# The second transform stage as four 64x64 TensorE tiles, with both filter products summed in PSUM

## The chip, the cores and the metric

The kernel runs on one core of one Trainium2 chip. The metric is the device time of one execution in microseconds, as the median of several runs. The engines named here are TensorE (PE, with its weight loads as PEld), VectorE (DVE), ScalarE (ACT), GpSimd (Pool) and SyncE (SP).

## The reference

The input `x` has 8 sequences of 3008 positions and 256 channels. Each channel is filtered along the sequence in the frequency domain, and every filtered position then goes through a two-layer MLP.

```python
def _attn_ref(x, filt_r, filt_i):                 # x (8, 3008, 256), filters (1505, 256)
    X = np.fft.rfft(x, axis=1)
    F = (filt_r + 1j * filt_i)[None, :, :]
    return np.fft.irfft(X * F, n=x.shape[1], axis=1).astype(np.float32)

def _moe_ref(x, w_in, w_out):                     # x (24064, 256), d_ff 2048
    h = x @ w_in
    return (np.maximum(0.01 * h, h) @ w_out).astype(np.float32)
```

## The kernel before

**The transform.** 3008 = 94 x 32. The real transform of a sequence is done in two stages of matmuls. Stage one (`s1_group`) multiplies the 94 rows of each of 32 positions `n2` with a twiddled matrix. Its output has four groups of 32 partitions: the real and imaginary parts for two halves of the 48 first-stage frequencies, 24 used partitions of 32 in each. A transpose of 32x32 blocks on DVE (`t1_part`) turns the layout, so that the 32 positions lie on partitions and the 24 frequencies on the free axis. Stage two (`s2_group`) multiplies this with `fwd2`, a 128x128 matrix. Only entries that join real and imaginary parts of one half of the frequencies are nonzero in it: two interleaved 64x64 blocks.

The spectrum is multiplied with the filter straight out of PSUM. `p1` is the spectrum times the real filter `fa`. `p2` takes the other half of the partitions (real and imaginary parts exchanged) times the imaginary filter `fb`. Pool adds the two into `y1`. The inverse runs the same way back: `sa_group` multiplies with `inv2` (128x128), ACT casts the result into the next layout (`spread`, L181), `t2_part` transposes on DVE, and `sb_group` multiplies with the inverse matrix of stage one and copies to `yts`, which is already the transposed input of the MLP.

**The MLP.** 47 chunks of 512 tokens. `moe1_group` (L365) fills one two-bank PSUM tile `ph` with four matmuls of 512 columns, and ACT applies the leaky ReLU (L370). `moe2_slice` (L379) makes eight matmuls of 256 columns into `po_ps`; after every second slice ACT copies the output (L386) and SP stores it.

**PSUM.** Two tiles `ph` of two banks, three tiles `pf` of one bank, one bank `po_ps`: all eight. `bank("pf", ...)` hands out the three `pf` tiles in turn, to every transform stage.

**Order.** The schedule is written out by hand. A slot is one `moe1_group`, then the transform work that is listed for that slot, then one `moe2_slice` of the chunk before:

```python
for slot in range(SL * (NCHUNK + 1)):
    ci, g = divmod(slot, SL)
    if ci < NCHUNK:
        moe1_group(ci, g)
    for f in tasks.get(slot, ()):
        f()
    if ci > 0:
        moe2_slice(ci - 1, g)
```

`plan` spreads the transform of batch b+1 over the slots of batch b. Its last arguments for the second stage are the first slot `s2`, the pace `step` in quarters of a slot, and `lag`, the slots between a group's forward part and its inverse part. Batch 1 has step 4, the others step 5, all lag 3. Each engine runs its instructions in the order in which the code issues them.

**The first batch** has no MLP work to hide behind. Its transform is done in two halves of the channels (`hf`), with functions of its own (`first_s1`, `first_s2`, `first_sa`, `first_t2`, `first_sb`). There both products already go to the inverse separately: `first_sa` multiplies one with `inv2` and the other with `inv2x` into one accumulation. Part of the products is made on Pool from ACT's copies of the spectrum, the rest on DVE. `upper` (L308) copies the filter from the lower 64 partitions to the upper 64, for one half of the channels: `fa` on ACT, `fb` on DVE. `first_sb` (L301) works in tiles of 64 columns, in pairs. `keep_warm` (L313) issues matmuls whose result nobody reads. Once the first batch is through, Pool flips the sign of the upper half of `fb` (L347), as the later batches want it.

**DMAs.** Pool's queue carries `x`, the filters (`filt_load`, L140) and the weights, one after another; SP's carries the constants and the output.

Of the kernel before, what the change touches and what calls it, by code (L numbers as in the profile page):

```python
# [10 lines left out]
P = 128  # L11
FP16 = mybir.dt.float16
# [7 lines left out]
NC = 24  # L20
Q = 32
# [4 lines left out]
def _build_np_constants(N):  # L26
    n1, n2 = np.arange(N1), np.arange(N2)
    h = N2 // 2

    k2 = np.concatenate([np.arange(h), np.arange(N2 - 1, h - 1, -1)])  # L30

    sg = np.where(k2 < h, 1.0, -1.0)[None, :]
    th = 2 * np.pi * np.outer(n2, k2) / N2
    co, si = np.cos(th), np.sin(th)

    fwd1 = np.zeros((R1, N2, P))
    inv1 = np.zeros((P, N2, N1))
    fwd2, inv2 = np.zeros((P, P)), np.zeros((P, P))

    for s, (qr, qi) in enumerate(((0, 2), (1, 3))):  # L40
        k1 = NC * s + np.arange(NC)

        w = np.where((k1 == 0) | (k1 == N1 // 2), 1.0, 2.0)[:, None] / N1
        for j in n2:
            ang = 2 * np.pi * (np.outer(n1, k1) / N1 + j * k1[None, :] / N)
            fwd1[:N1, j, qr * Q : qr * Q + NC] = np.cos(ang)
            fwd1[:N1, j, qi * Q : qi * Q + NC] = -np.sin(ang)
            inv1[qr * Q : qr * Q + NC, j, :] = w * np.cos(ang).T
            inv1[qi * Q : qi * Q + NC, j, :] = -w * np.sin(ang).T

        cr, ci = (slice(64 * i + s, 64 * i + 64, 2) for i in range(2))
        r, i = (slice(Q * q, Q * q + Q) for q in (qr, qi))
        fwd2[r, cr], fwd2[i, cr] = co, si
        fwd2[r, ci], fwd2[i, ci] = -si * sg, co * sg
        inv2[cr, r], inv2[ci, r] = co.T, -(si * sg).T
        inv2[cr, i], inv2[ci, i] = si.T, (co * sg).T
    inv2 /= N2

    inv2x = np.concatenate([inv2[64:], -inv2[:64]], axis=0)
    small = np.stack([fwd2, inv2, inv2x], axis=1)  # L60
    fwd1 = fwd1.reshape(R1, FP, N2 // FP, P).transpose(1, 0, 2, 3)
    return (np.ascontiguousarray(fwd1).astype(np.float16), inv1.astype(np.float16), small.astype(np.float16))
# [3 lines left out]
def kernel(  # L66
# [16 lines left out]
    CH = 512  # L83
# [12 lines left out]
    small_sb = cpool.tile([P, 3, P], FP16, name="small_sb")  # L96
    fa_sb = cpool.tile([P, NC, D], FP16, name="fa_sb")
    fb_sb = cpool.tile([P, NC, D], FP16, name="fb_sb")
# [8 lines left out]
    ypp = ctx.enter_context(tc.tile_pool(name="ypp", bufs=4))  # L107
# [98 lines left out]
    def s2_group(b, g):  # L206
        def go():
            ps = bank("pf", 2, D)
            src = big[(4 * b + 1) % 3][:].rearrange("p (n d) -> p n d", n=Q)
            nc.tensor.matmul(ps, fwd2, src[:, ds(2 * g, 2), :], start=True, stop=True)  # L210
# [5 lines left out]
            nc.vector.tensor_tensor(p2[64:P], ps[0:64], fb[0:64], AL.mult)  # L216
            y1 = ypp.tile([P, 2, D], FP16, tag="y", name=f"y_b{b}_g{g}")
            nc.gpsimd.tensor_tensor(y1[:], p1[:], p2[:], AL.add)  # L218
            ys[(b, g)] = y1
        return go  # L220

    def sa_group(b, g):
        def go():
            ps = bank("pf", 2, D)
            nc.tensor.matmul(ps, inv2, ys.pop((b, g))[:], start=True, stop=True)  # L225
            spread(big[(4 * b + 2) % 3], 2 * g, ps, nc.scalar.copy)
        return go
# [28 lines left out]
    def first_s2(hf, c, n, on_pool):  # L256
        ps = bank("ph", n, DH)
        src = paired(big[1])
        for j in range(0, n, 4):
            nc.tensor.matmul(ps[:, ds(j, 4), :].rearrange("p n (e t) -> p n e t", t=2), fwd2,  # L260
                             src[:, ds(c + j, 4), ts(hf, DH // 2)], start=True, stop=True)
        fs = [f[:, ds(c, n), ts(hf, DH)] for f in (fa_sb, fb_sb)]
        if on_pool:
            y = [outp.tile([P, n, DH], FP16, tag="ost", name=f"fy{i}_h{hf}_c{c}") for i in range(2)]
            xs = [scrp.tile([P, 4, DH], FP32, tag=f"p{j // 4 + 1}", name=f"fx_h{hf}_c{c + j}")
                  for j in range(0, n, 4)]
            for j, xf in enumerate(xs):
                act(xf[:], ps[:, ts(j, 4), :])
            for i in range(2):
                for j, xf in enumerate(xs):  # L270
                    nc.gpsimd.tensor_tensor(y[i][:, ts(j, 4), :], xf[:], fs[i][:, ts(j, 4), :], AL.mult)
        else:
            y = [ypp.tile([P, n, DH], FP16, tag=f"yw{i}", bufs=2, name=f"fy{i}_h{hf}_c{c}")
                 for i in range(2)]
            for i in range(2):
                nc.vector.tensor_tensor(y[i][:], ps, fs[i], AL.mult)  # L276
        ys[(hf, c)] = y

    def first_sa(hf, c):
        y = ys.pop((hf, c))  # L280
        for j in range(0, y[0].shape[1], 4):
            ps = bank("pf", 4, DH)
            for i, m in enumerate((inv2, inv2x)):
                nc.tensor.matmul(ps, m, y[i][:, ds(j, 4), :], start=(i == 0), stop=(i == 1))  # L284
            act(paired(big[2])[:, ds(c + j, 4), ts(hf, DH // 2)],
                ps.rearrange("p n (t e) -> p n e t", t=2))
# [18 lines left out]

    def upper(hf):
        for t, cp in ((fa_sb, act), (fb_sb, dve)):
            cp(t[64:P, :, ts(hf, DH)], t[0:64, :, ts(hf, DH)])  # L308


    def keep_warm(n):
        for _ in range(n):
            nc.tensor.matmul(po_ps.rearrange("p a d -> p (a d)"), small_sb[:, 0, :],  # L313
                             i1_sb[:].rearrange("p a d -> p (a d)")[:, 0:512],
# [31 lines left out]

    nc.gpsimd.tensor_scalar(fb_sb[64:P], fb_sb[64:P], -1.0, None, AL.mult)  # L347
# [51 lines left out]
    def plan(b, s1, per, t1, s2, step, lag, t2, sb):  # L399
# [57 lines left out]
```

## Time and profile before

| what | before |
|---|---|
| median of three runs | 785.82 us (785.38 to 785.87) |
| the profiled execution, own time | 787.67 us |
| its span | 785.9 us |
| mean granted TensorE clock | 0.997 |
| TensorE busy | 763.0 us, 97% |
| ACT busy | 557.0 us, 71% |
| DVE busy | 365.1 us, 46% |
| Pool busy | 150.7 us, 19% |
| first MLP matmul (L365) | 45.56 us after the start |

The profile is of one execution, in microseconds from the start of its span. Busy time is the sum over an engine's instructions. A line such as "L210 PE MATMUL ... x84 | 31.8, 379 | 0.0" is a group: source line, engine, operation, written and read tiles, count, then busy time in us, mean ns of one, and the idle time of the engine just before them. A matmul's duration is its whole flight through the array; the next one starts before it ends. In the timeline a row is the start, the duration, the engine, the line and the operation; neighbours of one kind are merged, and a bracket tells the idle time before and what ended it.

### The profile page before, as it was taken

Reading aid. Unit: us, or ns where it says so; the run is one execution under the profiler, and the core shown is the slowest. Engines: PE = TensorE matmul, PEld = TensorE weight load, DVE = VectorE, ACT = ScalarE, POOL = GpSimd, SP = SyncE. Lnnn points to the kernel's source line nnn. Section 1 sums busy time; section 2 is a strip of 40 time slices with the busy share of each in tenths; the row PEclk is TensorE's granted clock in tenths of the full one; section 3 lists DMA queues with packets and bytes.
Section 4 is the critical chain, followed back from the end, with each engine's and each line's share of the span. In section 5 each row is a group of like instructions: output and inputs, shape, how many; then the busy total and the mean of one; then the engine's idle time right before and its main releaser. Section 6 shows DMA issues by size and latency. Waiting matters only on the chain.

```text
span 785.9 us, 13623 instructions
## 1 busy us (share of the span) xinstructions
PE 763.0 (97%) x5812; PEld 528.6 (67%) x5812; DVE 365.1 (46%) x459; ACT 557.0 (71%) x794; POOL 150.7 (19%) x122
## 2 busy tenths in 40 slices
PE   2799999999999999999999999999999999999998
PEld 1356677666776677866777667776677667676666
DVE  3869760784327652387316754078432765200000
ACT  3686768676687767877687775967668776666664
POOL 5773400240003400052001410024000340000000
PEclk9999999999999999999999999999999999999999
DMA  9943010501032010501014101050100101101111
GB/s 174 214 59 94 28 42 28 122 28 41 28 79 70 28 41 28 119 31 41 28 41 108 41 28 41 28 120 28 42 28 28 41 28 42 41 28 41 41 41 54
DMA packets 42013, 43.39 MB, mean 55 GB/s; under 512 B 14274, under 2 KB 40514, under 8 KB 41282
## 3 DMA queue, kind: packets, MB, share of 16 engines
q0 software_dynamic: 15760, 16.99, 13.2%
q1 hardware_dynamic: 26192, 25.53, 9.3%
q8 instruction: 45, 0.74, 0.4%
q14 instruction: 16, 0.13, 0.1%
HBM read 34.10 MB, written 24.64 MB: 75 GB/s over the span
## 4 chain that ended last, share of the span: by engine, by line
PE 93%; ACT 2%; issue 1%; DVE 0%; ACTq 0%; DVEq 0%
PE po_ps L379 41%; PE ph L365 40%; PE pf L170 3%; PE pf L237 2%; PE pf L210 2%; PE pf L225 2%; PE pf L379 1%; ACT big L181 1%; ACT gt_c L370 1%; PE pf L284 1%; PE ph L260 0%; PE ph L301 0%; DVE fy_h_c L276 0%; PE po_ps L313 0%; PE pf L301 0%
## 5 line engine op out<-in xcount | busy, mean ns | idle before, releaser
L370 ACT ACTIVATE gt_c<-ph 128x1024 f16<-128x1024 f32 x376 | 384.8, 1024 | 194.8 <-PE ph L365 193.8
L365 PE MATMUL ph<-yt,w_in_sb 128*128 128x512 f16 (+7 forms) x1728 | 386.6, 351 | 0.4 <-ACT yt L304 0.2
L379 PE MATMUL po_ps<-w_out_sb,gt_c 128*128 128x256 f16 x2944 | 381.5, 272 | 0.6 <-ACT ost_c_t L386 0.6
L379 PEld LDWEIGHTS <-gt_c 128*128 128x128 f16 x3008 | 290.7, 98 | 86.7 <-issue 1.7
L365 PEld LDWEIGHTS <-w_in_sb 128*128 128x128 f16 x1728 | 163.0, 98 | 95.2 <-issue 1.0
L218 POOL TENSOR_TENSOR y_b_g<-p_b_g,p_b_g 128x512 f16<-128x512 f32 x84 | 106.9, 1273 | 225.5 <-DVE p_b_g L216 225.5
L181 ACT CAST big<-pf 128x512 f16<-128x512 f32 x195 | 111.8, 606 | 11.8 <-PE pf L251 11.7
L193 DVE STREAM_TRANSPOSE big<-big 128x1024 f32<-128x1024 f32 x32 | 55.8, 1846 | 127.1 <-ACT big L181 126.7
L240 DVE CAST yt<-pf 128x376 f16<-128x376 f32 x112 | 56.3, 545 | 85.9 <-PE pf L237 85.9
L214 DVE TENSOR_TENSOR p_b_g<-pf,fa_sb 128x512 f32<-128x512 f32 x84 | 58.1, 692 | 38.0 <-PE pf L210 35.5
L386 ACT COPY ost_c_t<-po_ps 128x256 f32<-128x256 f32 x184 | 69.4, 377 | 6.7 <-PE po_ps L379 5.6
L201 DVE STREAM_TRANSPOSE big<-big 128x1024 f32<-128x1024 f32 x28 | 51.1, 1936 | 34.5 <-ACT big L181 34.5
L215 DVE TENSOR_TENSOR p_b_g<-pf,fb_sb 64x512 f32<-64x512 f32 x84 | 58.2, 693 | 1.1
L216 DVE TENSOR_TENSOR p_b_g<-pf,fb_sb 64x512 f32<-64x512 f32 x84 | 57.4, 683 | 1.1
L132 POOL DMA_DIRECT2D x_sb<-in_x_dram x12 | 8.5, 713 | 256.6 <-PE pf L170 255.5
L237 PEld LDWEIGHTS <-big 128*128 128x128 f16 x448 | 25.7, 98 | 13.2
L170 PE MATMUL pf<-x_sb,f_sb 94*128 94x256 f16 x224 | 33.8, 272 | 0.1
L210 PE MATMUL pf<-big,small_sb 128*128 128x512 f16 x84 | 31.8, 379 | 0.0
L225 PE MATMUL pf<-y_b_g,small_sb 128*128 128x512 f16 x84 | 31.8, 379 | 0.0
L237 PE MATMUL pf<-i_sb,big 128*128 128x94 f16 x448 | 28.7, 206 | 0.0
L170 PEld LDWEIGHTS <-f_sb 94*128 94x128 f16 x224 | 21.0, 97 | 9.5 <-issue 1.3
L347 POOL TENSOR_SCALAR fb_sb<-fb_sb 64x6144 f16<-64x6144 f16 x1 | 15.7, 15742 | 0.4 <-DVE fy_h_c L276 0.4
(45 smaller groups left out, 142.8 us busy)
## 6 DMA issues: line engine op xcount, KB each, us to landing
out_dram<-ost_c_t SPq DMA_DIRECT2D x92, 256.0 KB, 2.1
x_sb<-in_x_dram POOLq DMA_DIRECT2D x6, 1536.0 KB, 11.3
x_sb<-in_x_dram POOLq DMA_DIRECT2D x4, 384.0 KB, 11.0
w_in_sb<-in_moe_w_in_dram POOLq DMA_DIRECT2D x1, 1024.0 KB, 14.9
w_out_sb<-in_moe_w_out_dram POOLq DMA_DIRECT2D x1, 1024.0 KB, 10.2
x_sb<-in_x_dram POOLq DMA_DIRECT2D x1, 1024.0 KB, 9.1
f_sb<-fwd_const SPq DMA_DIRECT2D x4, 192.0 KB, 3.2
fa_sb<-in_filt_r_dram POOLq DMA_DIRECT2D x4, 192.0 KB, 9.8
```

The lines of the kernel that those rows point to most:

```text
L170: nc.tensor.matmul(ps[:, j, :], f1_sb[:N1, n2, :], x_sb[:N1, n2, :], start=True, stop=True)
L181: copy(paired(dst)[:, ds(n0, nn), ds(e0, de)], ps.rearrange("p n (e t) -> p n e t", t=2))
L214: nc.vector.tensor_tensor(p1[:], ps, fa, AL.mult)
L215: nc.vector.tensor_tensor(p2[0:64], ps[64:P], fb[64:P], AL.mult)
L216: nc.vector.tensor_tensor(p2[64:P], ps[0:64], fb[0:64], AL.mult)
L218: nc.gpsimd.tensor_tensor(y1[:], p1[:], p2[:], AL.add)
L237: nc.tensor.matmul(ps[:, j, :], src[:, dt, n2, :], i1_sb[:, n2, :], start=True, stop=True)
L240: copy(yv[:, :, ds(4 * h, 4)], ps.rearrange("p c a -> p a c"))
L365: nc.tensor.matmul(ph[:, j, ds(o, ln)], w_in_sb[:, dt, ts(ct, P)], yts[b % 2][:, dt, ds(lo, ln)], start=(dt == 0), stop=(dt == NDT - 1),)
L370: nc.scalar.activation(gts[ci][:, ds(2 * g, 2), :], ph, AF.Lrelu)
L379: nc.tensor.matmul(po, gts[ci][:, ct, ts(tj, P)], w_out_sb[:, ct, :], start=(ct == 0), stop=(ct == NCT - 1))
L386: nc.scalar.copy(ost[:, tj % 2, :], po)
```

## The change

The second stage and its inverse are split into independent 64x64 problems: partitions 0 to 63 now hold the first set of frequencies, real above imaginary, partitions 64 to 127 the second. `fwd2`, `inv2` and `inv2x` shrink to 64x64 and are stored twice, once for each half of the partitions. The 24 frequencies of the free axis are split into two halves of `NH` = 12 as well, and these go to the upper and lower half of the output partitions. A unit `u` so handles two frequencies of each half with four matmuls of 64 rows and 64 columns, into two banks: the row half decides the bank, the column half the partitions. DVE makes four products of 128x512 (two banks, two filters) in fp16 and nothing is added; `sa_group` sums the products by accumulating `inv2` and `inv2x`, with eight matmuls into two banks. `plan` issues six units of two banks where there were twelve groups of one.

The filter is loaded in four pieces in place of two, and `upper` copies twice 32 partitions in place of once 64. The sign flip on Pool is gone. The first batch's functions follow the same layout.

```diff
+    fwd2 = np.block([[co, -si * sg], [si, co * sg]])
+    inv2 = np.block([[co.T, si.T], [-(si * sg).T, (co * sg).T]]) / N2
+    inv2x = np.concatenate([inv2[Q:], -inv2[:Q]], axis=0)
+    small = np.tile(np.stack([fwd2, inv2, inv2x], axis=1), (2, 1, 1))
...
-    small_sb = cpool.tile([P, 3, P], FP16, name="small_sb")
-    fa_sb = cpool.tile([P, NC, D], FP16, name="fa_sb")
-    fb_sb = cpool.tile([P, NC, D], FP16, name="fb_sb")
+    small_sb = cpool.tile([P, 3, P // 2], FP16, name="small_sb")
+    fa_sb = cpool.tile([P, 2, NH, D], FP16, name="fa_sb")
+    fb_sb = cpool.tile([P, 2, NH, D], FP16, name="fb_sb")
...
-    ypp = ctx.enter_context(tc.tile_pool(name="ypp", bufs=4))
+    ypp = ctx.enter_context(tc.tile_pool(name="ypp", bufs=3))
...
     def filt_load(dst, src, d0, dn):
-        for q, first, sgn in ((0, 0, 1), (Q, N1, -1)):
-            nc.gpsimd.dma_start(
-                dst[q : q + Q, :, ds(d0, dn)],
-                bass.AP(tensor=src.tensor, offset=src.offset + first * D + d0,
-                        ap=[[N1 * D, N2 // 2], [sgn * NC * D, 2], [sgn * D, NC], [1, dn]]))
+        for h in range(2):
+            for q, first, sgn in ((0, NC * h, 1), (Q // 2, N1 - NC * h, -1)):
+                nc.gpsimd.dma_start(
+                    dst[64 * h + q : 64 * h + q + Q // 2].rearrange("p s n d -> p (s n) d")[:, :, ds(d0, dn)],
+                    bass.AP(tensor=src.tensor, offset=src.offset + first * D + d0,
+                            ap=[[N1 * D, N2 // 2], [sgn * D, NC], [1, dn]]))
...
-    def s2_group(b, g):
-        def go():
-            ps = bank("pf", 2, D)
+    def s2_group(b, u):
+        def go():
             src = big[(4 * b + 1) % 3][:].rearrange("p (n d) -> p n d", n=Q)
-            nc.tensor.matmul(ps, fwd2, src[:, ds(2 * g, 2), :], start=True, stop=True)
-            fa, fb = fa_sb[:, ds(2 * g, 2), :], fb_sb[:, ds(2 * g, 2), :]
-            p1 = scrp.tile([P, 2, D], FP32, tag="p1", name=f"p1_b{b}_g{g}")
-            p2 = scrp.tile([P, 2, D], FP32, tag="p2", name=f"p2_b{b}_g{g}")
-            nc.vector.tensor_tensor(p1[:], ps, fa, AL.mult)
-            nc.vector.tensor_tensor(p2[0:64], ps[64:P], fb[64:P], AL.mult)
-            nc.vector.tensor_tensor(p2[64:P], ps[0:64], fb[0:64], AL.mult)
-            y1 = ypp.tile([P, 2, D], FP16, tag="y", name=f"y_b{b}_g{g}")
-            nc.gpsimd.tensor_tensor(y1[:], p1[:], p2[:], AL.add)
-            ys[(b, g)] = y1
-        return go
-    def sa_group(b, g):
-        def go():
-            ps = bank("pf", 2, D)
-            nc.tensor.matmul(ps, inv2, ys.pop((b, g))[:], start=True, stop=True)
-            spread(big[(4 * b + 2) % 3], 2 * g, ps, nc.scalar.copy)
+            pss = [bank("pf", 2, D) for _ in range(2)]
+            for h in range(2):
+                for s in range(2):
+                    r = slice(64 * s, 64 * s + 64)
+                    nc.tensor.matmul(pss[s][64 * h : 64 * h + 64], fwd2[r],
+                                     src[r, ds(NH * h + 2 * u, 2), :], start=True, stop=True)
+            y = [ypp.tile([P, 2, 2, D], FP16, tag=f"y{i}", name=f"y{i}_b{b}_u{u}") for i in range(2)]
+            for s in range(2):
+                for i, f in enumerate((fa_sb, fb_sb)):
+                    nc.vector.tensor_tensor(y[i][:, s], pss[s], f[:, s, ds(2 * u, 2), :], AL.mult)
+            ys[(b, u)] = y
+        return go
+    def sa_group(b, u):
+        def go():
+            y = ys.pop((b, u))
+            pss = [bank("pf", 2, D) for _ in range(2)]
+            for i, m in enumerate((inv2, inv2x)):
+                for s in range(2):
+                    for h in range(2):
+                        r = slice(64 * h, 64 * h + 64)
+                        nc.tensor.matmul(pss[h][64 * s : 64 * s + 64], m[r], y[i][r, s],
+                                         start=(i == 0), stop=(i == 1))
+            for h in range(2):
+                spread(big[(4 * b + 2) % 3], NH * h + 2 * u, pss[h], nc.scalar.copy)
         return go
...
     def first_s2(hf, c, n, on_pool):
-        ps = bank("ph", n, DH)
+        ps = bank("ph", 8, DH).rearrange("p (s n) d -> p s n d", s=2)[:, :, :n]
         src = paired(big[1])
-        for j in range(0, n, 4):
-            nc.tensor.matmul(ps[:, ds(j, 4), :].rearrange("p n (e t) -> p n e t", t=2), fwd2,
-                             src[:, ds(c + j, 4), ts(hf, DH // 2)], start=True, stop=True)
-        fs = [f[:, ds(c, n), ts(hf, DH)] for f in (fa_sb, fb_sb)]
+        for h in range(2):
+            for s in range(2):
+                r = slice(64 * s, 64 * s + 64)
+                nc.tensor.matmul(ps[64 * h : 64 * h + 64, s].rearrange("p n (e t) -> p n e t", t=2),
+                                 fwd2[r], src[r, ds(NH * h + c, n), ts(hf, DH // 2)],
+                                 start=True, stop=True)
+        fs = [f[:, :, ds(c, n), ts(hf, DH)] for f in (fa_sb, fb_sb)]
         if on_pool:
-            y = [outp.tile([P, n, DH], FP16, tag="ost", name=f"fy{i}_h{hf}_c{c}") for i in range(2)]
-            xs = [scrp.tile([P, 4, DH], FP32, tag=f"p{j // 4 + 1}", name=f"fx_h{hf}_c{c + j}")
-                  for j in range(0, n, 4)]
-            for j, xf in enumerate(xs):
-                act(xf[:], ps[:, ts(j, 4), :])
+            y = [outp.tile([P, 2, n, DH], FP16, tag="ost", name=f"fy{i}_h{hf}_c{c}") for i in range(2)]
+            xs = [scrp.tile([P, n, DH], FP32, tag=f"p{s + 1}", name=f"fx_h{hf}_c{c}_s{s}")
+                  for s in range(2)]
+            for s, xf in enumerate(xs):
+                act(xf[:], ps[:, s])
             for i in range(2):
-                for j, xf in enumerate(xs):
-                    nc.gpsimd.tensor_tensor(y[i][:, ts(j, 4), :], xf[:], fs[i][:, ts(j, 4), :], AL.mult)
+                for s, xf in enumerate(xs):
+                    nc.gpsimd.tensor_tensor(y[i][:, s], xf[:], fs[i][:, s], AL.mult)
         else:
-            y = [ypp.tile([P, n, DH], FP16, tag=f"yw{i}", bufs=2, name=f"fy{i}_h{hf}_c{c}")
+            y = [ypp.tile([P, 2, n, DH], FP16, tag=f"y{i}", name=f"fy{i}_h{hf}_c{c}")
                  for i in range(2)]
             for i in range(2):
                 nc.vector.tensor_tensor(y[i][:], ps, fs[i], AL.mult)
         ys[(hf, c)] = y
-    def first_sa(hf, c):
-        y = ys.pop((hf, c))
-        for j in range(0, y[0].shape[1], 4):
-            ps = bank("pf", 4, DH)
+    def first_sa(hf, *cs):
+        parts, n = [(c, ys.pop((hf, c))) for c in cs], 0
+        pss = [bank("pf", 4, DH) for _ in range(2)]
+        for c, y in parts:
+            w = y[0].shape[2]
             for i, m in enumerate((inv2, inv2x)):
-                nc.tensor.matmul(ps, m, y[i][:, ds(j, 4), :], start=(i == 0), stop=(i == 1))
-            act(paired(big[2])[:, ds(c + j, 4), ts(hf, DH // 2)],
-                ps.rearrange("p n (t e) -> p n e t", t=2))
+                for s in range(2):
+                    for h in range(2):
+                        r = slice(64 * h, 64 * h + 64)
+                        nc.tensor.matmul(pss[h][64 * s : 64 * s + 64, ds(n, w)], m[r], y[i][r, s],
+                                         start=(i == 0), stop=(i == 1))
+            n += w
+        for h in range(2):
+            act(paired(big[2])[:, ds(NH * h + cs[0], 4), ts(hf, DH // 2)],
+                pss[h].rearrange("p n (t e) -> p n e t", t=2))
...
     def upper(hf):
         for t, cp in ((fa_sb, act), (fb_sb, dve)):
-            cp(t[64:P, :, ts(hf, DH)], t[0:64, :, ts(hf, DH)])
+            for r in (0, 64):
+                cp(t[r + Q : r + 2 * Q, :, :, ts(hf, DH)], t[r : r + Q, :, :, ts(hf, DH)])
...
-    first_s2(0, 8, 8, True)
-    first_s2(0, 0, 8, False)
-    first_s2(0, 20, 4, True)
-    first_s2(0, 16, 4, False)
+    first_s2(0, 4, 4, True)
+    first_s2(0, 0, 4, False)
+    first_s2(0, 10, 2, True)
+    first_s2(0, 8, 2, False)
     for g in range(8):
         first_s1(1, g, two[g % 4 == 3], dve if g in (3, 5, 7) else act)
     x_load(1)
     t1_part(0, 2, True)(), t1_part(0, 3, True)()
     upper(1)
-    first_sa(0, 0), first_sa(0, 16)
-    first_s2(1, 8, 8, True)
-    first_s2(1, 0, 8, False)
+    first_sa(0, 0)
+    first_s2(1, 4, 4, True)
+    first_s2(1, 0, 4, False)
     nc.gpsimd.dma_start(w_out_sb[:], moe_w_out.rearrange("(ct p) d -> p ct d", p=P))
-    first_sa(0, 8), first_sa(0, 20)
-    first_s2(1, 16, 8, False)
+    first_sa(0, 8, 10), first_sa(0, 4)
+    first_s2(1, 8, 4, False)
     first_sa(1, 0)
     first_t2(0), first_t2(1)
-    first_sa(1, 16), first_sa(1, 8)
+    first_sa(1, 8), first_sa(1, 4)
     first_t2(2), first_t2(3)
...
-    nc.gpsimd.tensor_scalar(fb_sb[64:P], fb_sb[64:P], -1.0, None, AL.mult)
...
-        for g in range(12):
-            at(s2 + (step * g) // 4, s2_group(b, g))
-            at(s2 + lag + (step * g) // 4, sa_group(b, g))
+        for u in range(NH // 2):
+            at(s2 + (step * u) // 2, s2_group(b, u))
+            at(s2 + lag + (step * u) // 2, sa_group(b, u))
```

More of the change, by code (lines that the diff above doesn't have):

```diff
@@ L20 @@
 NC = 24
+NH = NC // 2
 Q = 32
@@ L37, in _build_np_constants @@
     inv1 = np.zeros((P, N2, N1))
-    fwd2, inv2 = np.zeros((P, P)), np.zeros((P, P))
-    for s, (qr, qi) in enumerate(((0, 2), (1, 3))):
-        k1 = NC * s + np.arange(NC)
+    for s in range(2):
+        k1 = (NC * np.arange(2)[:, None] + NH * s + np.arange(NH)).reshape(NC)
         w = np.where((k1 == 0) | (k1 == N1 // 2), 1.0, 2.0)[:, None] / N1
+        r, i = (slice(Q * q, Q * q + NC) for q in (2 * s, 2 * s + 1))
         for j in n2:
             ang = 2 * np.pi * (np.outer(n1, k1) / N1 + j * k1[None, :] / N)
[L46 to L60, printed above, removed]
+            fwd1[:N1, j, r], fwd1[:N1, j, i] = np.cos(ang), -np.sin(ang)
+            inv1[r, j, :], inv1[i, j, :] = w * np.cos(ang).T, -w * np.sin(ang).T
+    fwd2 = np.block([[co, -si * sg], [si, co * sg]])
+    inv2 = np.block([[co.T, si.T], [-(si * sg).T, (co * sg).T]]) / N2
+    inv2x = np.concatenate([inv2[Q:], -inv2[:Q]], axis=0)
+    small = np.tile(np.stack([fwd2, inv2, inv2x], axis=1), (2, 1, 1))
     fwd1 = fwd1.reshape(R1, FP, N2 // FP, P).transpose(1, 0, 2, 3)
@@ L277, in first_s2 @@
         ys[(hf, c)] = y
[L279 to L286 removed]
+    def first_sa(hf, *cs):
[3 more added lines that the diff above has]
+            w = y[0].shape[2]
+            for i, m in enumerate((inv2, inv2x)):
+                for s in range(2):
+                    for h in range(2):
[6 more added lines that the diff above has]
+                pss[h].rearrange("p n (t e) -> p n e t", t=2))
     def first_t2(i):
@@ L307, in upper @@
         for t, cp in ((fa_sb, act), (fb_sb, dve)):
-            cp(t[64:P, :, ts(hf, DH)], t[0:64, :, ts(hf, DH)])
+            for r in (0, 64):
+                cp(t[r + Q : r + 2 * Q, :, :, ts(hf, DH)], t[r : r + Q, :, :, ts(hf, DH)])
     def keep_warm(n):
         for _ in range(n):
-            nc.tensor.matmul(po_ps.rearrange("p a d -> p (a d)"), small_sb[:, 0, :],
-                             i1_sb[:].rearrange("p a d -> p (a d)")[:, 0:512],
+            nc.tensor.matmul(po_ps.rearrange("p a d -> p (a d)"), i1_sb[:].rearrange("p a d -> p (a d)")[:, 0:P],
+                             i1_sb[:].rearrange("p a d -> p (a d)")[:, 0:CH],
                              start=True, stop=True)
```

## The prediction, made before the change was run

> **What bounds the kernel now.** I read the page first: busy time (part 1), the slices (part 2), the chain that ended last (part 4).
>
> ```profile
> PE 763.0 (97%) x5812; PEld 528.6 (67%) x5812; DVE 365.1 (46%) x459; ACT 557.0 (71%) x794; POOL 150.7 (19%) x122
> ...
> PE   2799999999999999999999999999999999999998
> ...
> PE 93%; ACT 2%; issue 1%; DVE 0%; ACTq 0%; DVEq 0%
> PE po_ps L379 41%; PE ph L365 40%; PE pf L170 3%; PE pf L237 2%; PE pf L210 2%; PE pf L225 2%; PE pf L379 1%; ACT big L181 1%; ACT gt_c L370 1%; PE pf L284 1%; PE ph L260 0%; PE ph L301 0%; DVE fy_h_c L276 0%; PE po_ps L313 0%; PE pf L301 0%
> ```
>
> TensorE is busy from the second slice to the last and carries 93% of the chain. DVE and Pool carry next to nothing: Pool's adds, 106.9 us in the groups, set no end. So two stages count separately: the steady stage, where every TensorE hole goes straight into the span, and the start before the first MoE matmul (45.56 us), where ACT, DVE and TensorE hand work to one another.
>
> The groups by line give the removed work:
>
> ```profile
> L218 POOL TENSOR_TENSOR y_b_g<-p_b_g,p_b_g 128x512 f16<-128x512 f32 x84 | 106.9, 1273 | 225.5 <-DVE p_b_g L216 225.5
> L210 PE MATMUL pf<-big,small_sb 128*128 128x512 f16 x84 | 31.8, 379 | 0.0
> L225 PE MATMUL pf<-y_b_g,small_sb 128*128 128x512 f16 x84 | 31.8, 379 | 0.0
> L308 ACT COPY fa_sb<-fa_sb 64x3072 f16<-64x3072 f16 x2 | 5.5, 2751 | 0.0
> ```
>
> No idle time stands before L210 or L225: the transform never waits today. 379 ns is the whole flight of a matmul; what it takes from the stream is the distance between starts, read in the timeline of one steady slot (the one with an inverse L225 and a forward L210):
>
> ```profile
> 262.59 0.38 PE L225 MATMUL pf<-y_b_g,small_sb 128*128 128x512 f16 x1
> 262.79 1.02 ACT L370 ACTIVATE gt_c<-ph 128x1024 f16<-128x1024 f32 x1 [0.38 <-PE ph L365]
> 262.81 0.38 PE L210 MATMUL pf<-big,small_sb 128*128 128x512 f16 x1
> 263.02 1.04 PE L379 MATMUL po_ps<-w_out_sb,gt_c 128*128 128x256 f16 x8
> ...
> 263.71 0.61 ACT L181 CAST big<-pf 128x512 f16<-128x512 f32 x1
> 263.90 1.03 PE L365 MATMUL ph<-yt,w_in_sb 128*128 128x512 f16 x4
> ```
>
> Starts at 262.59, 262.81, 263.02: 0.216 us per 512 columns. The eight L379 take 0.88, the four L365 0.86. ACT is in order: the activation of the slot's MoE half starts 0.2 after the last L365 gave way (262.59), holds ACT 0.92, and only then comes the cast that frees the inverse's bank, done at 264.32, 1.73 after 262.59.
>
> **The steady sum. Matmuls.** Before: 168 matmuls x 0.216 = 36.3 us. After: per unit of four frequencies one forward quad and two inverse quads (fb's product adds the second), each four 64x64 matmuls of 512 columns; 42 units x 3 = 126 quads. No row shows row tiles, so I bound a quad: 0.216 if the four run side by side, 0.86 if one after another. The nearest row is the first batch's inverse, 64-column tiles in pairs:
>
> ```profile
> 42.08 0.30 PE L301 MATMUL ph<-i_sb,big 128*64 128x94 f16 x3
> 42.31 0.82 PE L313 MATMUL po_ps<-i_sb,small_sb 128*128 128x512 f16 x3
> 43.06 0.69 PE L301 MATMUL pf<-i_sb,big 128*64 128x94 f16 x16
> 43.56 0.67 PE L301 MATMUL ph<-i_sb,big 128*64 128x94 f16 x16
> ```
>
> Sixteen matmuls of 94 columns take 0.50, 31 ns each, where 512 columns at 0.216 make 94 cost 0.040: the halves do run together. In the change each row half writes a bank of its own. I take 0.216: 27.2 us, a gain of 9.1.
>
> On this price the Trainium skill, "TensorE: Matmul & The Clock Gate", section "Part 3: Packing small matmuls — row/col tiling", says that tiles of different rows and columns start about 4 ns apart and that 16 of them gave 10.6 times the speed. By it a quad costs some 12 ns more at most, an estimate of 1.5 us over 126; no run here shows it.
>
> **Changes of tiling.** Three L313 need 3 x 0.216 = 0.65, but L301 starts 0.75 after the first: 0.10 lost on entry. On exit, the last three L301 start from 42.08 and L313 at 42.31: 0.23 less 3 x 31 ns leaves 0.14. So 0.24 for a visit to the small tiles, which lie between L365 and L379 every time. Visits: for b=1 forward and inverse units have separate slots, 12 visits; for b=2 to 7 forward units stand at slots 0, 2, 5, 7, 10, 12 and inverse units at 3, 5, 8, 10, 13, 15 from the stage's start, 10 visits each. 72 x 0.24 = 17.3 us; I take 16 (an exit behind 512 columns has less to catch up than one behind 94). Bounds: nothing, if the array changes while it streams, and 0.33 a visit (23.5 us), if each side waits out the flight that the 379 ns have beyond 216.
>
> The Trainium skill speaks against the change here: "TensorEngine Tiling (Array Packing)", section "Tiling Modes", says that changing the mode, not only the tile, drains TensorE. It gives no time; with the some 128 array cycles of drain in "TensorE: Matmul & The Clock Gate" (section "Step-by-step: what each phase is for"), two drains a visit are about 0.107 us, an estimate of 7.7 us over the 72, half of what the rows give; the rows decide.
>
> **A bank that isn't free.** A unit now takes two of the three pf banks at once, an inverse unit two as well. At offsets 5 and 10 of b=2 to 7 the inverse stands just ahead of a forward unit: four banks from three. The fourth is the inverse's first, and it is free only when ACT has cast it. Counting from the last L365 giving way: entry 0.10 and two quads put TensorE at the forward unit's second matmul at 0.54; by the slot above ACT is through the activation at 1.12 and through the cast at 1.73. TensorE stands 1.2 us; queued behind are the rest of the unit, L379 and the next slot's L365, all that sets the end. 2 x 6 x 1.2 = 14.4 us. Bounds: 0 if the bank were free, 1.6 each (19 us) if an output copy (L386, 377 ns) comes first.
>
> Other bank meetings are covered, narrowly. An inverse one slot behind a forward unit needs its first bank after two DVE products: matmul flight 0.45 and 2 x 0.70 = 1.85 after the unit's start; TensorE comes there at 0.22 + 0.14 + 0.88 + 0.86 + 0.10 = 2.20. If DVE is later than that 0.3, each of these 23 places (three in a batch, five for b=1) costs what is missing: inside the high end.
>
> **DVE, Pool, ACT.** Three products (692, 693, 683 ns) per two frequencies become four per four: DVE falls by 84 x 2.07 - 168 x 0.69 = 58 us, Pool loses 106.9 and the sign flip's 15.7 (L347). None ended a TensorE wait, so nothing comes back; the next x load leaves Pool earlier but was never waited for. ACT keeps as many casts.
>
> **The start.** The filter's upper copies become two of 32 partitions in place of one of 64. L214 on 128 partitions and L215 on 64 take the same 692 and 693 ns, so time goes by elements: ACT pays 2.75 more per half, DVE 0.96.
>
> ```profile
> 26.29 2.75 ACT L308 COPY fa_sb<-fa_sb 64x3072 f16<-64x3072 f16 x1
> 29.06 1.58 ACT L285 CAST big<-pf 128x512 f16<-128x512 f32 x3
> 30.50 1.12 ACT L268 COPY fx_h_c<-ph 128x512 f32<-128x512 f32 x2
> ```
>
> In the first half some 0.4 of it shows (the DVE product that started at 19.64 waits for ACT until 20.04). In the second, ACT is free at 26.7 + 5.5 = 32.2; two casts and two copies to 34.5, two casts of the next inverse (35.1, 35.7); that frees the bank for the one after, TensorE at 36.0, the last forward unit at 36.4, DVE's products 36.6 to 39.05, and L292 starts there where it started at 36.97: 2.1 late. The halved TensorE time in this stretch is inside this. Eight filter DMAs become sixteen; each issue costs Pool up to 0.71, and the reuse of its eight semaphores delays its first multiply from 19.39 to about 23.3. Its products of that half are then ready near 30, their inverse can't run before 32.8: hidden. If not, 3 us more. I take +2.1, bounds 0 and 5.
>
> **Sum.** -9.1 + 16.0 + 14.4 + 2.1 = +23.4. The profiled execution took 787.67, its span 785.9 and 1.8 around it, 1.85 above the median of 785.82. On the span: 809.3; on the median, 809.2. The case's own range, from its terms: 799 to 821.
>
> **Rivals.** *Two by two.* Only column halves share the array (that alone is seen), the row halves follow: 0.43 a quad, +27.2, 836.4. For it: no row shows row tiles. Against: each row half has its own bank and rows. One after another would be +82, which L301 speaks against.
>
> *No bank wait.* The cast comes early enough: 809.2 - 14.4 = 794.8, still slower. Against: ACT's order, activation first, in the slot above.
>
> *The array works ahead* (not slower). TensorE takes up loads and matmuls of free tiles past a waiting one, so neither drain nor bank holds the stream: -9.1 + 2.1, 778.8. For it: weight loads already run beside matmuls (528.6 us of PEld). It decides once both waits together stay under 7.0 us, 0.10 per visit. Against: the 0.10 and 0.14 at L313 are in the trace, and every matmul there starts in program order.
>
> **Chances.** 0.68 for the sum; two by two 0.12; no bank wait 0.11; working ahead 0.08; 0.01 beyond. A measurement tells about 0.2% (1.6 us) from no change. Faster 0.07, same 0.02, slower 0.91. The range 793 to 838 leaves out little but the working ahead.
>
> **What would show it.** Right: the four forward matmuls start within some 20 ns, quads 0.216 apart; a hole of 0.1 ahead of the first quad and of the first L379 behind it; twelve waits of about 1.2 for an ACT cast at the forward line; ACT's upper copies four of 2.75; the first MoE matmul near 47.7. Wrong: starts of a quad 0.1 or more apart (two by two), no wait of TensorE for ACT, or visits with no holes.

## The result, and the profile after

| what | before | after |
|---|---|---|
| median | 785.85 us (785.38 to 787.37) | 814.41 us (814.02 to 814.62) |
| profiled execution, span | 785.9 us | 812.5 us |
| first MoE matmul | 45.56 us | 47.97 us |
| from there to the end of the span | 740.3 us | 764.6 us |
| DVE busy / Pool busy | 365.1 / 150.7 us | 298.0 / 34.2 us |

The change makes the kernel slower: 1.0359 times the time, interval 1.0341 to 1.0377, or 28.6 us by the medians. The forecast was 809.2 us, range 793 to 838.

The page of the changed kernel, busy time and the chain:

```profile
PE 775.9 (95%) x6196; PEld 517.8 (64%) x6196; DVE 298.0 (37%) x377; ACT 562.2 (69%) x797; POOL 34.2 (4%) x47
...
PE 92%; ACT 3%; issue 3%; DMA 1%; DVE 1%; POOL 0%; ACTq 0%; DVEq 0%; POOLq 0%
```

DVE has lost 67 us of work and Pool 116, and nothing of it came back: TensorE carried the chain before and carries it now. What TensorE does less of (fewer columns in the stream) is eaten by time in which it streams nothing. The waits name one part of that, the groups the other:

```profile
PE pf L209 <- ACT big L175: 10.0, 12, 0.9
```

```profile
L209 PE MATMUL pf<-big,small_sb 64*64 64x512 f16 x168 | 21.7, 396 | 10.0 <-ACT big L175 10.0
L209 PEld LDWEIGHTS <-small_sb 64*64 64x64 f16 x168 | 6.0, 103 | 29.6 <-issue 28.4
L226 PEld LDWEIGHTS <-small_sb 64*64 64x64 f16 x336 | 6.1, 104 | 17.8 <-issue 17.8
```

L209 is now the forward line, L226 the inverse. The wait column counts from the end of a matmul's flight, so 12 waits of 0.83 are 1.2 us each in the stream. The timeline of one joint slot (all engines; weight loads left out where they say the same) shows all of it:

```profile
160.72 0.38 PE L378 MATMUL ph<-yt,w_in_sb 128*128 128x512 f16 x1
...
161.03 0.63 PE L226 MATMUL pf<-y_b_u,small_sb 64*64 64x512 f16 x8
161.14 1.02 ACT L383 ACTIVATE gt_c<-ph 128x1024 f16<-128x1024 f32 x1 [0.78 <-PE ph L378]
...
161.49 0.38 PE L209 MATMUL pf<-big,small_sb 64*64 64x512 f16 x1
162.06 1.09 ACT L175 CAST big<-pf 128x512 f16<-128x512 f32 x2
162.69 0.41 PE L209 MATMUL pf<-big,small_sb 64*64 64x512 f16 x3 [0.83 <-ACT big L175]
...
163.03 1.05 PE L392 MATMUL po_ps<-w_out_sb,gt_c 128*128 128x256 f16 x8
```

The last L378 starts at 160.72 and would give way at 160.94; the first tile starts at 161.03: 0.09 lost on entry. Eight inverse matmuls (two quads) take from 161.03 to 161.49; inside a quad the starts lie 3 ns apart. One forward matmul starts at 161.49. The next needs the inverse's first bank; ACT runs the activation first (161.14), casts from 162.06, and TensorE goes on at 162.69. L392 follows 0.34 after that, where a quad alone takes 0.22.

### The profile page after: what moved, and what is told of

Its sections match the earlier page's. It is cut to its first block, busy times and chain, and to the rows that moved or that the text cites. A ratio compares the mean times of both kernels' runs of the same rounds, so it can differ in the third digit from the quotient of the medians.

```text
span 812.5 us, 14182 instructions
## 1 busy us (share of the span) xinstructions
PE 775.9 (95%) x6196; PEld 517.8 (64%) x6196; DVE 298.0 (37%) x377; ACT 562.2 (69%) x797; POOL 34.2 (4%) x47
## 4 chain that ended last, share of the span: by engine, by line
PE 92%; ACT 3%; issue 3%; DMA 1%; DVE 1%; POOL 0%; ACTq 0%; DVEq 0%; POOLq 0%
PE po_ps L392 40%; PE ph L378 39%; PE pf L164 3%; PE pf L240 2%; PE pf L226 2%; PE pf L209 2%; ACT big L175 1%; DMA x_sb<-in_x_dram 1%; PE pf L392 1%; ACT fa_sb L323 1%; PE pf L294 0%; PE pf L254 0%; DVE fy_h_c L282 0%; ACT gt_c L383 0%; PE po_ps L328 0%
## 5 line engine op out<-in xcount | busy, mean ns | idle before, releaser
L378 PE MATMUL ph<-yt,w_in_sb 128*128 128x512 f16 (+7 forms) x1728 | 386.6, 351 | 0.4 <-ACT yt L317 0.2
L392 PE MATMUL po_ps<-w_out_sb,gt_c 128*128 128x256 f16 x2944 | 382.2, 273 | 0.5 <-ACT ost_c_t L399 0.5
L392 PEld LDWEIGHTS <-gt_c 128*128 128x128 f16 x3008 | 284.7, 98 | 93.3 <-issue 26.4
L378 PEld LDWEIGHTS <-w_in_sb 128*128 128x128 f16 x1728 | 163.0, 98 | 95.2 <-issue 1.2
L175 ACT CAST big<-pf 128x512 f16<-128x512 f32 x195 | 106.6, 605 | 9.9 <-PE pf L254 9.8
L214 DVE TENSOR_TENSOR y_b_u<-pf,fa_sb 128x512 f16<-128x512 f32 x84 | 57.6, 686 | 117.3 <-PE pf L209 88.9
L214 DVE TENSOR_TENSOR y_b_u<-pf,fb_sb 128x512 f16<-128x512 f32 x84 | 57.1, 680 | 0.0
L164 PE MATMUL pf<-x_sb,f_sb 94*128 94x256 f16 x224 | 33.8, 272 | 0.1
L209 PE MATMUL pf<-big,small_sb 64*64 64x512 f16 x168 | 21.7, 396 | 10.0 <-ACT big L175 10.0
L226 PE MATMUL pf<-y_b_u,small_sb 64*64 64x512 f16 x336 | 26.3, 388 | 0.0
L209 PEld LDWEIGHTS <-small_sb 64*64 64x64 f16 x168 | 6.0, 103 | 29.6 <-issue 28.4
L226 PEld LDWEIGHTS <-small_sb 64*64 64x64 f16 x336 | 6.1, 104 | 17.8 <-issue 17.8
L254 PE MATMUL pf<-x_sb,f_sb 94*128 94x128 f16 x40 | 5.0, 310 | 9.6 <-DMA x_sb<-in_x_dram 9.6
## 6 DMA issues: line engine op xcount, KB each, us to landing
x_sb<-in_x_dram POOLq DMA_DIRECT2D x6, 1536.0 KB, 10.9
```

The source lines that it names most:

```text
L164: nc.tensor.matmul(ps[:, j, :], f1_sb[:N1, n2, :], x_sb[:N1, n2, :], start=True, stop=True)
L175: copy(paired(dst)[:, ds(n0, nn), ds(e0, de)], ps.rearrange("p n (e t) -> p n e t", t=2))
L214: nc.vector.tensor_tensor(y[i][:, s], pss[s], f[:, s, ds(2 * u, 2), :], AL.mult)
L226: nc.tensor.matmul(pss[h][64 * s : 64 * s + 64], m[r], y[i][r, s], start=(i == 0), stop=(i == 1))
L378: nc.tensor.matmul(ph[:, j, ds(o, ln)], w_in_sb[:, dt, ts(ct, P)], yts[b % 2][:, dt, ds(lo, ln)], start=(dt == 0), stop=(dt == NDT - 1),)
L392: nc.tensor.matmul(po, gts[ci][:, ct, ts(tj, P)], w_out_sb[:, ct, :], start=(ct == 0), stop=(ct == NCT - 1))
```

## Experiments

Two of them change the number of joint slots, one does the arithmetic part of the change alone, three price a tile by itself, five look at the start, one at ACT's order. The line numbers are those of each kernel.

**No joint slot.**

```diff
-        plan(b, z, 2, z + 9, z + 13, 5, 3, z + 32, z + 37)
+        plan(b, z, 2, z + 9, z + 13, 5, 4, z + 32, z + 37)
```

> The changed kernel with lag 4 in place of 3 for batches 2 to 7: forward units stay at offsets 0, 2, 5, 7, 10, 12, inverse units go to 4, 6, 9, 11, 14, 16, so no slot holds both. Theory (the fourth bank is not free, about 1.26 us for each of the 12 joint slots): these waits vanish, -15.1 us, and 12 more visits to the small tiles come, 12 x 0.2 = +2.4: about 801.7. Rival (the joint slot is slow for another reason, or the wait moves to the next slot's bank): 810 to 815, with waits of TensorE for ACT or DVE at the forward or the inverse line.

Measured: 801.28 us, 1.0204 of the kernel before (1.0186 to 1.0222). No wait of L209 for ACT is left. From the first MoE matmul to the last matmul's start it takes 747.8 in place of 760.5 us: -12.7, as worked out (-15.1 + 2.4).

**Four joint slots** (the same edit with lag 5).

> The changed kernel with lag 5: inverse units of batches 2 to 7 at 5, 7, 10, 12, 15, 17, so four joint slots per batch in place of two, 24 in all. Theory (bank wait): 12 more waits of 1.26 us, +15.1, and 12 visits fewer, -2.4: about 827. Rival (visits are what costs, the joint slot saves one): about 812.

Measured: 826.23 us, ratio 1.0509 (1.0488 to 1.053). The waits doubled in number and sum, each as long as before:

```profile
PE pf L209 <- ACT big L175: 20.0, 24, 0.9
```

The time follows the number of joint slots (0, 2, 4 per batch: 801, 814, 826) and not the number of visits, which goes the other way (84, 72, 60). The wait for the fourth bank is shown as a cause, with its price.

**The sum in PSUM alone, on the whole array**, built on the kernel before:

```diff
-            nc.vector.tensor_tensor(p1[:], ps, fa, AL.mult)
-            nc.vector.tensor_tensor(p2[0:64], ps[64:P], fb[64:P], AL.mult)
-            nc.vector.tensor_tensor(p2[64:P], ps[0:64], fb[0:64], AL.mult)
...
-            nc.gpsimd.tensor_tensor(y1[:], p1[:], p2[:], AL.add)
...
+            for i, f in enumerate((fa, fb)):
+                nc.vector.tensor_tensor(y[:, i], ps, f, AL.mult)
...
-            nc.tensor.matmul(ps, inv2, ys.pop((b, g))[:], start=True, stop=True)
...
+            for i, m in enumerate((inv2, inv2x)):
+                nc.tensor.matmul(ps, m, y[:, i], start=(i == 0), stop=(i == 1))
```

> The kernel before with one part of the change alone: both products kept in fp16 and summed in the inverse's accumulation (inv2 and inv2x on the full 128x128 array), two DVE products per group in place of three, no Pool add and no sign flip; no tiles, one bank per group as before. Theory (TensorE is the bound, DVE and Pool end no wait): 84 more matmuls x 0.216 = +18.1, about 804. Rival (DVE's 58 us and Pool's 123 us give something back): below 800.

Measured: 803.61 us, ratio 1.0228 (1.021 to 1.0247): +18.0. Taking the add off Pool costs just the 84 matmuls that replace it. The freed engines, off the path here, give nothing back. The lag 4 kernel, with no bank wait either, does the same sum with tiles in 801.3, longer start included: the tiles earn back only a little of it.

**One visit to a smaller tile, by itself**, in the kernel before. The edit, for 64x64; the others differ in rows and columns:

```diff
+        if ci < NCHUNK and slot >= 48 and slot not in tasks:
+            ps = bank("pf", 1, CH)[:, 0, :]
+            nc.tensor.matmul(ps[0:64], small_sb[0:64, 0, 0:64],
+                             i1_sb[:].rearrange("p a d -> p (a d)")[0:64, 0:CH],
+                             start=True, stop=True)
```

> The kernel before with one more matmul of 512 columns on a 64x64 tile, whose result nobody reads, in each of the 90 slots from slot 48 on that hold no transform work. Theory (each visit to a smaller tile costs about 0.09 on entry and 0.09 to 0.12 on exit): the first L379 behind it starts 0.31 to 0.33 us after it, and it starts 0.31 after the last L365; 90 x (0.216 + 0.2) = +37, about 823. Rival (the price belongs to four tiles or to the reading of the spectrum, not to the change of tiling): 90 x 0.216 = +19, about 805.

> The kernel before with the 90 unread matmuls of 512 columns, on 64 rows and all 128 columns. Theory (any change of the tile's shape stops the stream): entry 0.31, exit 0.31 to 0.33 between starts as with 64x64; about 823. Rival (only splitting columns does): the stream runs on at 0.216, about 805.

> The kernel before with the 90 unread matmuls of 512 columns on all 128 rows and 64 columns. Theory (any smaller tile stops the stream on entry and on exit): starts 0.31 after the last L365 and 0.31 to 0.33 before the first L379, about 823. Rival (splitting columns alone costs less, since all rows stay in one): under 0.25 on one side, 815 or less.

| tile (rows x columns) | start after the last L365 | next L379 after it | time |
|---|---|---|---|
| 64 x 64 | 0.309 us | 0.332 us | 822.61 |
| 64 x 128 | 0.312 us | 0.319 us | 824.51 |
| 128 x 64 | 0.309 us | 0.336 us | 823.23 |

The table's distances are medians over 90 visits; 0.216 is what the stream takes without a change. Each time is a single run and holds its start; from the first MoE matmul to the end of the span the three take 778.3, 777.3 and 778.6 us, against 740.3 without the visits. The timeline of TensorE with the 64x64 tile, at one of its visits:

```profile
207.43 1.03 PE L365 MATMUL ph<-yt,w_in_sb 128*128 128x512 f16 x4
208.39 0.40 PE L427 MATMUL pf<-i_sb,small_sb 64*64 64x512 f16 x1
208.72 1.05 PE L379 MATMUL po_ps<-w_out_sb,gt_c 128*128 128x256 f16 x8
209.60 1.03 PE L365 MATMUL ph<-yt,w_in_sb 128*128 128x512 f16 x4
```

Four L365 give way at 208.29, the tile starts at 208.39; it gives way at 208.61, L379 starts at 208.72. So 0.2 us per visit belongs to the change of tiling, whichever side is split, with one matmul or with twelve.

What holds the stream there is not shown. Two rows bear on it: the weight load of an inverse matmul in the kernel before, which starts 0.21 ahead of its matmul (262.59), and the load of the first tiles in the changed kernel, which starts only with its matmul (161.03):

```profile
262.38 0.10 PEld L225 LDWEIGHTS <-small_sb 128*128 128x128 f16 x1
```

```profile
161.03 0.14 PEld L226 LDWEIGHTS <-small_sb 64*64 64x64 f16 x8 [0.42 <-issue]
```

An array that must run empty and weights that cannot be loaded ahead both fit these rows, and no run separates them.

**The start: TensorE's clock.** `warm(n)` issues n matmuls of 512 columns that nobody reads.

```diff
+    warm(11)
     for g in range(8):
+        if g == 4:
+            warm(2)
         first_s1(0, g, two[(g // 2) % 2], (act, dve)[g % 2])
...
+    warm(8)
```

(and 2, 6, 3, 2 and 3 ahead of later steps.)

> The changed kernel with matmuls that nobody reads (94 to 96 rows, 512 columns, on the constants that have landed) in TensorE's holes of the start: 11 before the first input lands, and 2 to 8 in each later wait, 37 in all. Theory (the start is long because TensorE stays at the lower clock until 41.9 us, where the kernel before has the full one from about 26): the granted clock is full before 15 us, the matmuls of the start halve, and the first MoE matmul comes at 44 to 45.5 in place of 47.6 to 48; about 811.5. Rival (ACT's two further filter copies set the start): not before 47; about 814.

Measured: 814.67 us, first MoE matmul at 49.23. It does not tell the theories apart: the full clock came at 26.9 and was lost again from 33.8 to 44.0, the stretch that matters. These times are those of the trace's clock records. The first record of a trace grants the full clock; ahead of it the profile's rows print 1.00 for want of a record, and the lower clock is read from the distance of two matmuls of 512 columns, 0.43 us in place of 0.216. A second try put the matmuls only into that stretch:

> The changed kernel with 24 unread matmuls only where the start is long: in TensorE's holes between 26 and 40 us (6, 6, 5, 2 and 5, of 512 columns). Measured from the landing of the second input piece to the first MoE matmul, which takes the DMA's own changes out: 36.5 to 36.6 us in two profiles of the change so far, 32.0 to 33.2 with the start of the kernel before. Theory (the lower clock until 41.9 lengthens the last inverses and the keep-warm matmuls): full clock by 34, distance 35 or less, about 812.5. Rival (other engines set it): 36.5 or more, 814.5.

```diff
     first_sa(0, 0)
+    warm(6)
     first_s2(1, 4, 4, True)
     first_s2(1, 0, 4, False)
+    warm(6)
...
-    first_sa(0, 8, 10), first_sa(0, 4)
+    first_sa(0, 8, 10)
+    warm(5)
+    first_sa(0, 4)
     first_s2(1, 8, 4, False)
+    warm(2)
     first_sa(1, 0)
+    warm(5)
```

Measured: 812.79 us (814.45 for the kernel without ACT's copy, below, on the same chip), the full clock from 25.7 on, and 34.6 us from the landing of the second input piece (10.73) to the first MoE matmul (45.37), where the change has 36.6. The keep-warm matmuls of the original code tell the clock, first in the changed kernel, then in this one (timelines of TensorE and of all engines):

```profile
39.17 1.06 PE L294 MATMUL pf<-fy_h_c,small_sb 64*64 64x512 f16 x7 [0.32 <-ACT big L298]
40.17 2.09 PE L328 MATMUL po_ps<-i_sb 128*128 128x512 f16 x5
42.19 0.69 PE L314 MATMUL pf<-i_sb,big 128*64 128x94 f16 x16
```

```profile
37.85 0.62 PE L294 MATMUL pf<-fy_h_c,small_sb 64*64 64x512 f16 x7 [0.52 <-ACT big L298]
38.40 1.25 PE L328 MATMUL po_ps<-i_sb 128*128 128x512 f16 x5
39.59 0.69 PE L314 MATMUL pf<-i_sb,big 128*64 128x94 f16 x16
```

Five L328 last 2.09 against 1.25: their starts lie 0.427 apart, then 0.216. In every profile of the changed kernel and its variants but this one L328 runs at half rate, in every profile with the old first stage the same matmuls run at the full one. The quads finish the first batch's inverses in half the stream, TensorE has more holes, and it stays at the lower clock until 41.9. Three profiles with the old first stage (sum in PSUM alone, the 64x64 and the 128x64 visit) have the full clock from 26.1 to 26.6 on; two others, that of the kernel before among them, have it from 27.2 and 26.5, lose it for 3.4 us and have it back at 34.0 and 33.3. Filling the holes is worth about 1.9 us of the start, 1.7 by the medians.

**The same matmuls in the kernel before** (11, 2, 8, 2 and 4, at the places of the first try).

> The kernel before with the same idle matmuls in the holes of its start (27 of them). Theory (the clock counts there too): full clock before 15 us, first MoE matmul at 40 to 41.5 in place of 42.5 to 45.6; about 783.5. Rival (DMA landings, ACT and DVE set that start): no difference, 785.6.

Measured: 785.45 against 785.84 us, ratio 0.9998 (0.9989 to 1.0006), first MoE matmul at 42.14. The full clock was there from 7.8 to 18.1 and from 24.9 on. No difference is shown: the interval leaves the clock at most 0.9 us in that start. It was the one idea for a kernel faster than both, and it isn't.

**ACT's added copy, moved to DVE.**

```diff
-        for t, cp in ((fa_sb, act), (fb_sb, dve)):
-            for r in (0, 64):
+        for t, cps in ((fa_sb, (act, dve)), (fb_sb, (dve, dve))):
+            for r, cp in zip((0, 64), cps):
```

> The changed kernel with one of ACT's two filter copies per half moved to DVE (one of fa's two on ACT, the other three copies on DVE). Theory (ACT's further copies of 2.75 us set the start): first MoE matmul at 45 to 46 in place of 47.6 to 48; about 812.5. Rival (the clock sets it): 47 or later; about 814.

Measured: 817.78 us, ratio 1.0401 (1.0375 to 1.0427), with runs from 814.65 to 819.4 worse than the change, first MoE matmul at 52.37. The theory fell, and the rival's 814 too; one reason is in neither: DVE's copies meet Pool's products. DVE's timeline, then Pool's:

```profile
29.62 2.44 DVE L323 COPY fa_sb<-fa_sb 32x3072 f16<-32x3072 f16 x1
32.09 5.14 DVE L323 COPY fb_sb<-fb_sb 32x3072 f16<-32x3072 f16 x2
37.27 1.23 DVE L282 TENSOR_TENSOR fy_h_c<-ph,fa_sb 128x1024 f16<-128x1024 f32 x1
```

```profile
30.58 2.00 POOL L277 TENSOR_TENSOR fy_h_c<-fx_h_c_s,fb_sb 128x256 f16<-128x256 f32 x2
32.53 0.60 POOL L125 DMA_DIRECT2D x_sb<-in_x_dram  x1
33.15 2.27 POOL L277 TENSOR_TENSOR fy_h_c<-fx_h_c_s,fa_sb 128x512 f16<-128x512 f32 x2
37.31 2.27 POOL L277 TENSOR_TENSOR fy_h_c<-fx_h_c_s,fb_sb 128x512 f16<-128x512 f32 x2 [1.89 <-DVE fb_sb L323]
```

In the changed kernel two such copies take 1.94 in the first half, before Pool's first product, and 2.54 in the second, beside its products; here three took 7.6. The clock may have a part in it: it was at half from 30.5 to 47.6, where the changed kernel has the full one from 41.9. This run does not separate the two.

**ACT's added copy, left out.** So it was taken away instead; fa's last 32 partitions are zero and that part of the product is missing.

```diff
+    nc.vector.memset(fa_sb[96:P], 0.0)
...
+                if t is fa_sb and r == 64:
+                    continue
```

> The changed kernel without one of ACT's two filter copies per half: fa's last 32 partitions stay zero, so that part of the filter product is left out. Theory (ACT's added copy of 2.75 us per half delays its casts, and through the three banks everything behind): the distance from the second input piece to the first MoE matmul falls from 36.5 to 34 to 34.5; about 812. Rival (TensorE's clock or Pool's late products set it): 36 or more, about 814.

Measured: 814.45 us, ratio 1.0368 (1.0349 to 1.0387) where the change has 1.0359, distance 36.5: no gain. The theory fell. The chain of this kernel between 11 and 49 us, by line, says what stands beside ACT:

```profile
by line: DMA x_sb<-in_x_dram 25.2%; DMA fa_sb<-in_filt_r_dram 22.3%; POOL fy_h_c L278 18.6%; PE pf L295 11.4%; PE po_ps L331 7.5%; PE ph L315 6.7%; issue 5.9%; POOL x_sb L125 5.1%; PE pf L315 4.5%; DVE fy_h_c L283 3.3%; ACT big L299 3.1%; P
```

ACT's copy is gone from it, and Pool's products, late behind the filter's sixteen DMAs, hold the same step: the last of the first half ends at 33.23, the inverse starts at 33.27. In the changed kernel Pool's last product of the first half ends at 31.73, the inverse that needs it starts at 31.86, ACT's cast ahead of it ends at 31.8: two chains of the same length. Taking both away was not tried.

**ACT's output copy.** In the lag 4 kernel the second cast of an inverse unit goes to DVE:

```diff
-                spread(big[(4 * b + 2) % 3], NH * h + 2 * u, pss[h], nc.scalar.copy)
+                spread(big[(4 * b + 2) % 3], NH * h + 2 * u, pss[h], (act, dve)[h])
```

> The change with lag 4 and the second cast of each inverse unit on DVE in place of ACT. Theory (two casts in a row push ACT's output copy back, and L392 waits for its bank in some slots that have no such wait in the kernel before): the sum of those waits falls from 2.07 us in the lag 4 profile to the 1.3 of the kernel before; about 800.5, no more than a small step. Rival (DVE's casts come late behind its products and hold a bank): 802 or more, with waits of TensorE for DVE at the forward line.

Measured: 800.97 us, not to be told from 801.28. In the profile the excess over the stream in the starts from the last L378 to the first L392, in slots with no transform work on TensorE, falls from 2.07 us in eleven slots to 1.03 in three; the changed kernel has 2.84, the kernel before 1.29. From the first MoE matmul to the last matmul's start it takes 746.8 in place of 747.8: the 1.0 comes back there, though it is too small for the medians. The wait looks like this in the changed kernel:

```profile
181.71 1.09 ACT L175 CAST big<-pf 128x512 f16<-128x512 f32 x2
182.12 1.03 PE L378 MATMUL ph<-yt,w_in_sb 128*128 128x512 f16 x4
182.67 0.40 ACT L399 COPY ost_c_t<-po_ps 128x256 f32<-128x256 f32 x1
183.12 1.03 PE L392 MATMUL po_ps<-w_out_sb,gt_c 128*128 128x256 f16 x8
```

L378 gives way at 182.98, L392 waits until 183.12 for the output copy, which stands behind two casts in a row.

## Why the prediction was right, and where it was not

| term of the sum | predicted | measured |
|---|---|---|
| matmuls, 126 quads for 168 | -9.1 | -7.2 |
| changes of tiling, 72 visits | +16.0 | +14.3, +0.7 in the L392 behind |
| fourth bank, 12 waits | +14.4 | +14.5 |
| ACT's output copy behind two casts | none | +1.5 |
| end of the span after the last matmul | none | +0.5 |
| start | +2.1 | +2.4 to the profile, about +4.3 to the median |

The measured steady terms are sums over the starts of the profile: 93 ns on entry, 116 on exit from a forward unit and 92 from an inverse one, 10 more in the second L392; an inverse takes 0.466 for two quads, a forward unit 0.226. The visits and waits without those 10 ns come to +21.4 directly; the rounded rows add to 21.6.

The mechanism was the forecast one, term by term, in sign and nearly in size. *Quads*: side by side, 3 ns apart, so "two by two" is out; but the last tile starts 10 ns behind the first (the forecast named 12 as an estimate and left them out of the sum), and the first of two quads takes 0.24; that is the missing 1.9. *Tiling*: the two rows around L313 gave 0.24 per visit and the value taken was 0.22; 0.20 was right, and it holds for tiles split in rows alone, which no row had shown. The estimate of 7.7 us from the 128 cycles of drain in the Trainium skill ("TensorE: Matmul & The Clock Gate", section "Step-by-step: what each phase is for") was half of it. *Bank*: ACT's order in one slot gave 1.2, and 1.20 it is; "no bank wait" and "working ahead" are out: the forward matmuls for the free bank stood behind the blocked one.

Pool's and DVE's freed time came back nowhere, as said, and the sum in PSUM alone shows it on a kernel of its own.

Two steps of the sum failed. *The start*, taken at 2.1, is 4.3 by the medians: 28.6 less the 24.2 between first MoE matmul and end. The profile of before hid half of the difference, because its own start was late: 45.56 us, where three other profiles with that first stage have 42.5 to 42.9 and one 45.46. In the two late ones the second input piece landed at 12.4 and 12.5 in place of 10.5 to 10.9, and the clock was lost for 3.4 us. So it is in part luck that the 47.97 after lies so near the forecast 47.7. From the second input piece's landing to the first MoE matmul it is 32.0 to 33.2 against 36.5 to 37.3 us. The sum had "the halved TensorE time in this stretch is inside this" as a gain; it was a loss, since the idler TensorE kept the lower clock (1.9 us, shown by filling its holes). "Hidden" for Pool was wrong too: its products came at 31.73, not near 30, just as late as ACT's casts, and their inverse started at 31.86, not after 32.8. How the other 2.5 us split between these two chains stays open. *ACT's casts*: the sum said that ACT "keeps as many casts" and left it there; two in a row delay the copy queued behind them, 1.5 us; with lag 4, moving one of the two to DVE took 1.0 of these waits away.

The quads, the casts, the end and the start came out 1.9, 1.5, 0.5 and 2.2 us dearer than forecast, the visits 1.0 cheaper: that makes the 5.2 us between 809.2 and 814.4. Why the span ends 0.5 us later after the last matmul stays open. The "own range, 799 to 821" has no working: the bounds given for the terms add up to 777 to 824.

## What to carry to other kernels

Splitting the array into tiles pays by the stream time saved per visit: here a unit saved 0.86 - 0.69 = 0.17 us of matmuls and paid about 0.2 for each of its two visits between full-size matmuls. The way out would be to collect tile work until a visit saves well over the price of going in and out (not tried here), and to count the PSUM banks it then holds at once: two units of two banks from a pool of three cost 1.2 us each time, six times a visit's price. Taking work off engines that ended no wait was worth nothing here, and putting it on the one that did cost its full price.

## What the hardware showed that was not expected

A DVE copy of 32x3072 fp16 within SBUF takes 0.97 us alone. In the kernel with three copies on DVE, one took 2.44 beside Pool's products and the next 4.16; the third took 0.95, while Pool stood still. Pool loses as well: a product of 128x256 that takes 0.66 took 1.37 beside a copy. (The 1.89 that Pool waits in its rows is another thing: it waits for the filter half that DVE is copying.) The Trainium skill, "SBUF — State Buffer", section "Who interferes with whom", says that DVE's fast copies and GpSimd need one shared port pair and that the loser waits for the whole instruction; these rows agree with it in kind. The copy of 4.16 ended 0.83 after the second of two products in a row, so it stood still for more than one of Pool's instructions.

The clock does not follow from "TensorE has work": 37 extra matmuls had it full from 26.9 to 33.8 and lost it for the next 10 us, while 24 others placed in the late holes kept it from 25.7 on. The same eleven matmuls ahead of the first input had it full at 7.8 us in the kernel before and not before 26.9 in the changed one. Each of these is one profile.
